# Attention, a cosine layer and a routed expert layer: the first layer from pairs of 256-token blocks to single blocks of 384 tokens, with weight bits in PSUM and a shorter gate

## Chip, cores, metric

The kernel runs on one core of one Trainium2 chip. The time is the device time of one execution in microseconds; it was run three times. A core has TensorE (matrix products, PE in the profile, its weight loads PEld), VectorE (DVE), ScalarE (ACT), GpSimd (POOL) and SyncE (SP), which here issues DMAs. Each engine works through its own queue in order.

## The reference

Three layers one after the other, all in float32:

```
x = attention(q, k, v)            # 4 batches, 8 heads, 576 positions, head size 64; the first 4 heads see a band
                                  # of 32 positions back, the last 4 see 32 positions in steps of 4
h = x @ w_in                      # 2304 tokens x 512 -> 2048
x = (h * cos(h)) @ w_out          # -> 512
logits = x @ w_gate + log1p(exp(x @ w_noise)) * noise      # 8 experts
top2, weights = the two largest of each token, softmax over them
out[token] += weight * relu(x @ w1[e]) @ w2[e]             # for both experts of a token; 512 -> 1024 -> 512
```

## The kernel before

**Precision.** A product in full float32 is made of three products in a faster float32 format: each operand is split into a rounded part and a rest (`PASSES`, L45), high with high, high with low, low with high. So every operand costs a rounding copy on ScalarE and a subtraction on VectorE or GpSimd. Small products (scores, transposes, gate) are plain float32; each of them, except the transposes, stands twice in the trace.

**Attention** is done in 16 units `u` (one batch and one pair of heads each): load, `a_scores` (L404), `a_exp`, `a_norm`, three transposes and the product with v (`a_part`, L525). Its result, already transposed, goes into a ring of 768 tokens in SBUF, `xraw`. Units 0 to 3 run in the opening; the others are laid beside the steps of the first layer. `x_split` (L540) cuts a block of the ring into the two parts.

**The first layer** works on 9 blocks of 256 tokens, and on pairs `p` of hidden chunks of 128 (8 pairs). A step (`g1`, `post`, `g2`) is: 24 products of 256 columns into one PSUM tile of 512; the cosine on it (ScalarE, VectorE, ScalarE twice, VectorE, ScalarE, GpSimd); and, two steps later, 12 products of 512 columns into the sums of the block's two tiles of tokens. The order of the 72 steps (L732) is: blocks 0 and 1 in turn through the 8 pairs (16 steps), then blocks 2 to 8 one after the other. PSUM has eight banks: two for `ph`, two for `mid` (attention), four with the tag `acc`, for the sums.

**Weights of the first layer** come as 64-bit words. `w_load` brings a piece of 512 KB (four a pair), `w_bits` (L282) puts each number together from its two words with three VectorE operations in place in SBUF (L290 to L292), `w_parts` rounds it on ScalarE (L298) and takes the rest on GpSimd (L299). Four pieces are cut in the opening, the other 28 during the first sixteen steps. The last pair comes over the small tiles `piece`.

**What sets the order.** The list `BESIDE` (L57) says, by step and place in it, which functions are issued there: `8:0` is after step 8's first cosine half and before the rest. The loop (L982) issues a step's first products, the cosine in three stretches and the second products of the step two before, with those functions in between.

**Routing** of a block of 256: `r_rows` writes the sums out, `r_trans` transposes them (8 transposes), `r_gate` (L617) makes partial gate sums of 32 rows for each quarter of the 512 features, `r_logits` transposes these (2) and adds them up; then softplus, the two largest, and `r_rank`, which gives each token its place in its experts' lists by products with a triangle of ones; `r_send` scatters number and weight into the list `tab` in DRAM, two indirect DMAs for each tile of 128 tokens.

**The experts.** Each expert has 608 places, as tiles of 128, 128, 96 (the first part, 352) and 128, 128 (the second part, 256). For an expert: gather and transpose the rows, 8 times 12 products with w1 for each part (`m_g1`, L891), 24 products of 512 columns for each tile with w2 (`m_y`, L928), scale, and add into the output rows by indirect DMA. Expert 0's first part is read from the lists before the last two blocks are routed (`t_first`, L830); its hidden layer runs while the last block is routed (L1015 to L1023). What follows needs the last block's entries.

Of the kernel before, what the change touches and what calls it, by code (L numbers as in the profile page):

```python
# [9 lines left out]
F32 = mybir.dt.float32  # L10
# [20 lines left out]
TB = 256  # L31
NBLK = NT // TB
NPAIR = DFF // 256
# [5 lines left out]
CAP = CA + CB  # L39
NEG = -8e9  # L40
TWO_PI = 2.0 * math.pi
RING = 3 * TB
# [11 lines left out]
)  # L54

# [30 lines left out]
9:1 w_bits(5,3)  # L86
9:2 a_part(6,0)
10:0 w_parts(5,2)
10:1 w_parts(5,3) w_piece(7,1) a_part(6,1)
# [3 lines left out]
11:1 a_exp(7) w_bits(7,0) w_parts(6,3)  # L93
12:-1 a_norm(7)
12:0 w_bits(7,1) w_parts(7,0) w_piece(7,2)
12:1 w_parts(7,1)
12:2 w_piece(7,3)
13:-1 a_loadv(7)
13:0 a_loadqk(8) a_part(7,0)
14:1 a_part(7,1)  # L100
14:2 w_bits(7,2) w_bits(7,3) x_split(2,0,2) a_part(7,2) w_parts(7,2)
15:-1 w_parts(7,3) x_split(2,2,3,1)
15:0 x_split(2,3,4,1)
16:0 a_loadv(8)
# [12 lines left out]
24:-1 a_part(8,1) r_logits(0)
24:0 zero_out(2)
24:1 a_part(8,2) r_trans(1)
25:-1 a_part(9,0)  # L120
25:0 r_exp(0) r_top(0)
25:2 a_scores(10)
26:-1 r_top2(0) r_gate(1) a_loadv(9) a_part(9,1)
26:0 zero_out(5) a_loadqk(11) r_rows(2) r_pick(0)
26:1 a_part(9,2) a_exp(10) a_norm(10) r_trans(2)
26:2 a_scores(11)
27:-1 a_loadv(10) zero_out(4) zero_out(6)
27:0 r_logits(1) r_gate(2) r_exp(1)
27:1 a_part(10,0) zero_out(7)
28:-1 a_part(10,1)  # L130
28:0 a_part(10,2) r_rank(0)
28:2 r_top(1) r_top2(1) r_send(0,0) a_exp(11)
29:-1 a_loadqk(12) a_norm(11)
29:0 a_loadv(11)
29:1 r_send(0,1)
29:2 r_pick(1) a_part(11,0)
30:-1 zero_out(9) a_part(11,1) zero_out(8) r_logits(2)
30:0 a_part(11,2)
30:1 r_exp(2)
30:2 a_loadv(12) x_split(4) zero_out(10) r_top(2) r_top2(2)  # L140
31:2 r_rank(1) zero_out(11) r_pick(2)
32:0 r_send(1,0)
32:2 r_send(1,1) zero_out(12)
33:2 zero_out(13) r_rank(2) r_rows(3)
34:0 r_send(2,0)
34:2 zero_out(14) r_send(2,1) r_trans(3)
35:2 zero_out(15) r_gate(3)
36:2 a_scores(12) zero_out(16)
37:0 a_loadqk(13)
37:2 a_exp(12) zero_out(17) r_logits(3)  # L150
38:1 a_norm(12) r_exp(3)
38:2 a_scores(13) x_split(5) r_top(3) r_top2(3)
39:0 a_part(12,0) a_loadqk(14)
39:2 a_part(12,1) a_exp(13) r_pick(3)
40:0 a_part(12,2)
40:1 a_norm(13)
40:2 a_loadv(13) a_scores(14)
41:0 a_part(13,0) a_loadqk(15)
41:2 a_part(13,1) a_exp(14) r_rank(3) r_rows(4)
42:0 a_part(13,2) r_send(3,0)  # L160
42:1 a_norm(14)
42:2 a_loadv(14) a_scores(15) r_send(3,1) r_trans(4)
43:0 a_part(14,0)
43:2 a_part(14,1) a_exp(15) r_gate(4)
# [1021 lines left out]
```

## Time and profile before

| | us |
|---|---|
| three timed runs | 1032.69, 1036.55, 1035.54; median 1035.54 |
| the profiled execution: its own time | 1032.98 |
| the profiled execution: span | 1031.2 |
| granted TensorE clock over the span | 0.984 of full speed |
| TensorE busy | 980.9 |
| VectorE, ScalarE, GpSimd busy | 547.5, 458.7, 368.1 |

"Busy" is the time in which an engine had at least one operation running; idle time stands beside the operation that followed it, with what ended the wait. The granted clock has two levels, 1.2 and 2.4 GHz; a mean of 0.93 says that a part of the stretch ran at the lower one.

### The profile page before, as it was taken

The page shows a single profiled execution, that of the slowest core. Times are in us where ns is not written, and L with a number is a line of the kernel's source. Part 1 is how long each engine was busy: PE and PEld are TensorE (multiplying, and loading weights), DVE is VectorE, ACT ScalarE, POOL GpSimd, SP SyncE. Part 2 cuts the span into 40 slices and gives each one's busy share as a digit, 9 for nine tenths or more (in the row PEclk, how much of TensorE's full clock was granted, in tenths as well). Part 3 has the DMA queues.
Part 4 walks back from the last instruction along what each step waited for, and adds up shares of the span by engine and source line. Part 5 has one row for each costly group of instructions (what it writes and reads, how often), then busy time and mean ns, then how long its engine had stood idle before and what let it go on. Part 6 is the DMA issues. An engine that isn't in the chain of part 4 may idle for free.

```text
span 1031.2 us, 16810 instructions
## 1 busy us (share of the span) xinstructions
PE 980.9 (95%) x6560; PEld 864.8 (84%) x6560; DVE 547.5 (53%) x1134; ACT 458.7 (44%) x908; POOL 368.1 (36%) x477
## 2 busy tenths in 40 slices
PE   8797989999999899999999889999999999999995
PEld 6676778988889788898887689898898979898984
DVE  7799885357754655354464556344453536353221
ACT  6646765555645655455554334233232414142110
POOL 5555553243453341323334432231313232322211
PEclk9998999999999999999999999999999999999998
DMA  9962212223312120000054345453434243441201
GB/s 216 328 220 81 80 55 43 85 72 114 96 52 57 40 55 1 21 1 23 21 192 122 84 134 176 140 168 110 156 126 157 76 154 124 157 149 55 67 26 47
DMA packets 70601, 105.19 MB, mean 102 GB/s; under 512 B 31251, under 2 KB 44819, under 8 KB 70512
## 3 DMA queue, kind: packets, MB, share of 16 engines
q1 hardware_dynamic: 60528, 76.34, 24.3%
q0 software_dynamic: 9984, 27.68, 8.7%
q8 instruction: 54, 0.88, 0.4%
q14 instruction: 35, 0.29, 0.1%
HBM read 85.41 MB, written 19.59 MB: 102 GB/s over the span
## 4 chain that ended last, share of the span: by engine, by line
PE 72%; DVE 13%; ACT 5%; DMA 4%; issue 3%; SPq 1%; POOL 1%; ACTq 0%; DVEq 0%; POOLq 0%
PE pe L903 20%; PE ye L938 20%; PE ph L562 13%; PE acc L589 12%; DVE cut L291 3%; DMA raw<-in_wm 2%; PE sc L430 2%; PE mgx L886 2%; DVE cut L290 1%; DVE cut L292 1%; DVE r L571 1%; PE mo L505 1%; DVE po L654 1%; PE mt L485 1%; DVE r L575 1%
## 5 line engine op out<-in xcount | busy, mean ns | idle before, releaser
L562 PE MATMUL ph<-xhl,wm 128*128 128x256 f32 x1728 | 230.0, 289 | 11.6 <-ACT wm L298 4.3
L562 PEld LDWEIGHTS ph<-xhl,wm 128*128 128x128 f32 x1728 | 219.4, 195 | 19.9 <-ACT wm L298 4.7
L938 PE MATMUL ye<-we,h 128*128 128x512 f32 (+1 forms) x960 | 231.0, 397 | 0.0
L589 PE MATMUL acc<-wm,g 128*128 128x512 f32 x864 | 220.3, 398 | 2.8 <-POOL wm L299 0.9
L938 PEld LDWEIGHTS ye<-we,h 128*128 128x128 f32 (+1 forms) x960 | 173.9, 184 | 43.3
L589 PEld LDWEIGHTS acc<-wm,g 128*128 128x128 f32 x864 | 156.8, 190 | 33.7 <-POOL wm L299 1.2
L579 POOL TENSOR_TENSOR g<-r,g 128x512 fp32r<-128x512 f32 x72 | 95.7, 1329 | 207.5 <-ACT g L578 207.4
L903 PE MATMUL pe<-xga,we 128*128 128x352 f32 x768 | 125.4, 323 | 0.0
L903 PEld LDWEIGHTS pe<-xga,we 128*128 128x128 f32 x768 | 122.7, 188 | 0.5 <-issue 0.4
L951 POOL DMA_INDIRECT out<-old,tir x35 | 35.6, 1017 | 221.9 <-DVE old L949 217.1
L906 DVE SCALAR_TENSOR_TENSOR h<-pe,h 128x256 fp32r<-128x256 f32 (+1 forms) x128 | 60.6, 474 | 97.1 <-ACT h L905 96.2
L905 ACT ACTIVATE h<-pe 128x256 fp32r<-128x256 f32 (+1 forms) x128 | 54.2, 424 | 122.2 <-PE pe L903 122.2
L949 DVE SCALAR_TENSOR_TENSOR old<-ye,wts,old 128x512 f32<-128x512 f32 (+1 forms) x35 | 26.3, 750 | 135.5 <-PE ye L938 135.5
L903 PE MATMUL pe<-xgb,we 128*128 128x256 f32 x768 | 95.9, 286 | 1.8 <-DVE xgb L889 1.3
L903 PEld LDWEIGHTS pe<-xgb,we 128*128 128x128 f32 x768 | 94.7, 195 | 2.5 <-DVE xgb L889 1.5
L571 DVE SCALAR_TENSOR_TENSOR r<-r,ph 128x512 f32<-128x512 int32 x72 | 49.1, 682 | 82.9 <-ACT r L570 82.8
L575 DVE SCALAR_TENSOR_TENSOR r<-r,ph 128x512 f32<-128x512 f32 x72 | 49.4, 686 | 82.2 <-ACT r L574 82.0
L820 DVE TENSOR_TENSOR we<-wraw,we 128x512 fp32r<-128x512 f32 x121 | 82.5, 691 | 3.6 <-ACT we L819 0.9
L819 ACT ACTIVATE we<-wraw 128x512 fp32r<-128x512 f32 x128 | 78.4, 623 | 3.2 <-issue 3.2
L573 ACT ACTIVATE r<-r 128x512 f32<-128x512 f32 x72 | 45.4, 631 | 65.5 <-DVE r L571 65.4
L570 ACT ACTIVATE r<-ph 128x512 int32<-128x512 f32 x72 | 42.6, 592 | 51.1 <-PE ph L562 50.9
L578 ACT ACTIVATE g<-r 128x512 fp32r<-128x512 f32 x72 | 45.4, 631 | 43.8 <-DVE r L575 29.5
(181 smaller groups left out, 1035.3 us busy)
## 6 DMA issues: line engine op xcount, KB each, us to landing
wraw<-in_we SPq DMA_DIRECT2D x64, 512.0 KB, 5.7
raw<-in_wm SPq DMA_DIRECT2D x28, 512.0 KB, 9.8
vts<-in_v SPq DMA_DIRECT2D x13, 384.0 KB, 3.9
x1d<-x SPq DMA_DIRECT2D x9, 512.0 KB, 3.6
out<-zt SPq DMA_DIRECT2D x18, 256.0 KB, 3.9
kts<-in_kT SPq DMA_DIRECT2D x13, 288.0 KB, 3.1
qts<-in_qT SPq DMA_DIRECT2D x26, 144.0 KB, 3.9
piece<-in_wm SPq DMA_DIRECT2D x4, 512.0 KB, 4.0
```

Of the source, the lines that this page charges most:

```text
L562: nc.tensor.matmul(ph[:, j, :], w[:, a, o:o + P], t[:, x, c, :], start=(c == 0 and n == 0 and (j == 0 or len(cs) == 4)), stop=(c == 3 and ...
L571: nc.vector.scalar_tensor_tensor(r, n, -TWO_PI, ph, op0=ALU.mult, op1=ALU.add)
L573: nc.scalar.activation(r, r, AF.Sin, scale=0.5)
L575: nc.vector.scalar_tensor_tensor(r, r, 0.5, ph, op0=ALU.subtract, op1=ALU.mult)
L579: nc.gpsimd.tensor_tensor(g[:, 1, :], r, g[:, 0, :].bitcast(F32), op=ALU.subtract)
L589: nc.tensor.matmul(ACC[blk][t], g[:, a, j * TB + t * P:j * TB + (t + 1) * P], w[:, x, 1024 + j * DM:1024 + (j + 1) * DM], start=(p == 0 an ...
L819: nc.scalar.activation(t[:, 0, fs], raw, AF.Copy)
L820: eng.tensor_tensor(t[:, 1, fs], raw, t[:, 0, fs].bitcast(F32), op=ALU.subtract)
L903: nc.tensor.matmul(ph[:, :n], w[:, a, o:o + P], x[:, b, c, :], start=(c == 0 and i == 0), stop=(c == 3 and i == 2))
L905: nc.scalar.activation(h[:, 0, f, :], ph[:, :n], AF.Relu)
L906: nc.vector.scalar_tensor_tensor(h[:, 1, f, :], ph[:, :n], 0.0, h[:, 0, f, :].bitcast(F32), op0=ALU.max, op1=ALU.subtract)
L938: nc.tensor.matmul(acc, h[:, a, f, o:o + n], w[:, b, (f % 4) * DM:(f % 4 + 1) * DM], start=(f == 0 and i == 0), stop=(f == 7 and i == 2))
```

## The change

- The first layer has 6 blocks of 384 tokens, and a step is one hidden chunk of 128 instead of two: 12 products of 384 columns, and, two steps later, 9 products of 512 columns into three sums. There are 96 steps, and the blocks run one after the other from the start.
- `x_split` works on one quarter of the features at a time, with six such tiles in turn.
- The four banks `acc` become four banks `k0` to `k3` that are given out by number. A block's three sums take three of them; the fourth serves its neighbour's routing, and, while weights are being cut, the intermediate of `w_bits`.
- The last pair of weights comes in eight pieces of half the size.
- For attention units 4 to 7, the scaling of the maxima and the copies of the result go from VectorE to ScalarE.
- The gate is one product per tile and quarter: the transposed rows are loaded, the 16 gate columns are streamed, and the four quarters add up in PSUM. `r_logits` goes away.
- Routing is done 6 times, for three tiles each.
- `t_first` reads the first parts of experts 0 and 1 before the last block is routed. Of expert 0's weights 14 of 16 splits run beside the steps. Expert 1's first rows are gathered while the last block is routed, and its first part's products stand before expert 0's second part.
- `BESIDE` is written anew from step 9 on.

```
-TB = 256
+TB = 384
-RING = 3 * TB
+RING = 2 * TB
...
     def w_bits(j, k):
...
+        b = bank(f"bits{j}_{k}", BITS[0]).bitcast(U32)[:, :n]
         V = nc.vector
-        V.tensor_scalar(t, hw, 3, 0x3FFFFFF8, op0=ALU.logical_shift_left, op1=ALU.bitwise_and)
-        V.scalar_tensor_tensor(t, hw, 0xC0000000, t, op0=ALU.bitwise_and, op1=ALU.bitwise_or)
-        V.scalar_tensor_tensor(t, lw, 29, t, op0=ALU.logical_shift_right, op1=ALU.bitwise_or)
+        V.tensor_scalar(b, hw, 3, 0x3FFFFFF8, op0=ALU.logical_shift_left, op1=ALU.bitwise_and)
+        V.scalar_tensor_tensor(b, hw, 0xC0000000, b, op0=ALU.bitwise_and, op1=ALU.bitwise_or)
+        V.scalar_tensor_tensor(t, lw, 29, b, op0=ALU.logical_shift_right, op1=ALU.bitwise_or)
...
+    def x_split(blk, c, eng=nc.vector):
+        t = bpool.tile([P, 2, TB], F32R, tag="xhl", name=f"xhl{blk}_{c}", bufs=6)
...
+    def g1(blk, f, cs=range(4)):
+        w, j = WM[f // 2], f % 2
...
+        for c in cs:
+            for n, (a, x) in enumerate(PASSES):
+                o = c * 256 + j * P
+                nc.tensor.matmul(ph, w[:, a, o:o + P], XHL[blk, c][:, x, :],
+                                 start=(c == 0 and n == 0), stop=(c == 3 and n == 2))
...
+    def g2(blk, f, ts=range(NTB)):
...
+        for t in ts:
+            for n, (a, x) in enumerate(PASSES):
+                nc.tensor.matmul(ACC[blk][t], g[:, a, t * P:(t + 1) * P],
+                                 w[:, x, 1024 + j * DM:1024 + (j + 1) * DM],
...
+    def r_gate(blk):
+        mid = r_bank(f"mg{blk}", blk)
+        for t in range(NTB):
             for c in range(4):
...
+                nc.tensor.matmul(mid[:, t * 2 * NE:(t + 1) * 2 * NE], RT[blk][t][:, c, :], wgn[:, c, :],
+                                 start=(c == 0), stop=(c == 3))
...
-    steps = [(blk, p) for p in range(NPAIR) for blk in range(2)]
-    steps += [(blk, p) for blk in range(2, NBLK) for p in range(NPAIR)]
+    steps = [(blk, f) for blk in range(NBLK) for f in range(NF)]
...
+    r_trans(LAST, 0)
+    r_trans(LAST, 1)
+    m_g1(0, 0, 0)
+    r_trans(LAST, 2)
+    split_we(0, 3, 2)
+    m_g1(0, 0, 1)
+    r_gate(LAST)
+    r_exp(LAST)
+    split_we(0, 3, 3)
     load_we(1, 0)
     load_we(1, 1)
+    m_g1(0, 0, 2)
+    r_top(LAST)
...
+    for t in range(3):
+        t_gather(1, t)
+    for f in range(5, 8):
+        m_g1(0, 0, f)
+    r_rank(LAST)
+    for t in range(NTB):
+        r_send(LAST, t)
+    for t in range(3):
+        m_y(0, t)
+        t_trans(1, t)
+        for q in range(3 * t, min(3 * t + 3, 8)):
+            split_we(1, q // 4, q % 4)
+    t_load(0, 2)
     t_gather(0, 3)
     t_gather(0, 4)
...
+    t_load(2, NE)
+    for f in range(8):
+        m_g1(1, 0, f)
+        if f == 5:
+            t_weights()
+            for t in range(3):
+                m_out(0, t)
     t_trans(0, 3)
     t_trans(0, 4)
```

## Rows read from the trace of the kernel before

**Rows 1.** The page, part 1: busy time, share of the span and instructions by engine

```profile
PE 980.9 (95%) x6560; PEld 864.8 (84%) x6560; DVE 547.5 (53%) x1134; ACT 458.7 (44%) x908; POOL 368.1 (36%) x477
```

**Rows 2.** Windows: stretch, length, busy PE, PEld, DVE, ACT, POOL; clock, DMA, GB/s

```profile
0.00:39.90 39.90, 34.26 (x355) 27.57 (x355) 28.10 (x63) 27.47 (x119) 20.45 (x49) 1.00 1.05 258
39.90:165.90 126.00, 109.06 (x766) 93.88 (x767) 110.31 (x149) 75.06 (x162) 71.07 (x57) 0.93 0.42 128
165.90:553.60 387.70, 379.28 (x2774) 335.56 (x2773) 205.25 (x550) 215.03 (x338) 140.43 (x164) 1.00 0.18 55
553.60:639.70 86.10, 79.12 (x462) 70.80 (x461) 48.09 (x111) 33.33 (x68) 34.53 (x48) 0.96 0.51 149
639.70:1031.20 391.50, 379.21 (x2208) 337.02 (x2206) 155.74 (x264) 107.78 (x224) 101.65 (x163) 0.99 0.35 114
```

**Rows 3.** Chain of waits: start us, us, what (instructions), single pieces of it

```profile
233.81 1.98 PE sc L430 x18
...
454.07 2.87 PE ph L562 x24
456.94 2.75 PE acc L589 x12
...
555.57 0.87 PE mx L613 x8
...
558.36 0.57 PE mg L621 x8
...
561.04 0.22 PE ml L630 x2
...
612.46 5.47 PE ye L938 x24
...
624.30 5.76 PE pe L903 x36
...
964.42 26.86 PE pe L903 x192
```

**Rows 4.** By line: duration ns min/median/max, first and last start, forms

```profile
L290 DVE TENSOR_SCALAR cut<-raw x28: 368/420/1521, 21.6 to 141.0; 128x512 uint32<-128x512 uint32 x28
...
L291 DVE SCALAR_TENSOR_TENSOR cut<-raw,cut x28: 691/1370/1685, 22.0 to 141.4; 128x512 uint32<-128x512 uint32 x28
...
L571 DVE SCALAR_TENSOR_TENSOR r<-r,ph x72: 627/686/689, 39.9 to 546.2; 128x512 f32<-128x512 int32 x72
```

**Rows 5.** Windows of what reads or writes `cut`: busy DVE, ACT, POOL

```profile
39.90:165.90 126.00, 81.44 (x84) 17.80 (x28) 36.95 (x29) 0.93 0.42 128
```

**Rows 6.** Waits of VectorE, 39.9 to 165.9: us in total, times, longest

```profile
DVE r L575 <- ACT r L574: 7.8, 6, 1.4
DVE r L571 <- ACT r L570: 5.9, 5, 1.6
```

**Rows 7.** Groups by line and shape: operations on 384 columns (busy us, mean ns)

```profile
L448 POOL TENSOR_TENSOR s<-s,mx 128x384 f32<-128x384 f32 x8 | 7.1, 886 | 0.1
...
L888 ACT ACTIVATE xga<-mgx 128x384 fp32r<-128x384 f32 x8 | 3.9, 490 | 28.6 <-PE mgx L886 28.6
L889 DVE TENSOR_TENSOR xga<-mgx,xga 128x384 fp32r<-128x384 f32 x8 | 4.4, 556 | 0.7
```

**Rows 8.** TensorE in order of time: start, us, what, idle before it

```profile
574.53 0.19 PE L693 MATMUL mr<-os,tri 128*128 128x8 bf16 x1 [3.73 <-DVE os L687]
...
592.06 0.66 PE L886 MATMUL mgx<-ident,xg 128*128 128x128 f32 x4 [0.30 <-DMA xg<-x1d,tic]
...
598.09 5.95 PE L903 MATMUL pe<-xgb,we 128*128 128x256 f32 x35 [1.32 <-DVE xgb L889]
```

**Rows 9.** GpSimd in order of time: start, us, what, idle before it

```profile
223.57 1.92 POOL L474 TENSOR_TENSOR s<-s,sm 128x288 f32<-128x288 f32 x3 [0.42 <-DVE sm L472]
...
577.08 1.17 POOL L714 DMA_INDIRECT tab<-pay,si  x1 [5.80 <-DVE si L707]
...
581.63 0.95 POOL L714 DMA_INDIRECT tab<-pay,si  x1 [0.23 <-issue]
```

More of the change, by code (lines that the diff above doesn't have):

```diff
@@ new lines @@
+47:-1 x_split(3,2)
+47:0 x_split(3,3)
+47:2 a_exp(14) a_loadqk(15)
+48:0 a_norm(14)
+49:0 a_part(14,0)
+49:2 a_part(14,1) r_rows(2)
+50:0 a_part(14,2) r_trans(2,0)
+50:2 a_scores(15) r_trans(2,1)
+51:0 r_trans(2,2) a_loadv(15)
+51:2 r_gate(2) a_exp(15)
+52:0 a_norm(15)
+52:1 r_exp(2)
+52:2 r_top(2) r_top2(2)
+53:0 a_part(15,0)
+53:2 a_part(15,1) r_pick(2)
+54:0 a_part(15,2) x_split(4,0)
+55:0 x_split(4,1)
+55:2 r_rank(2)
+56:0 r_send(2,0)
+56:2 r_send(2,1)
+57:0 r_send(2,2)
+63:-1 x_split(4,2)
@@ new lines @@
+63:0 x_split(4,3)
+65:2 r_rows(3)
+66:0 r_trans(3,0)
+66:2 r_trans(3,1)
+67:0 r_trans(3,2)
+67:2 r_gate(3)
+68:1 r_exp(3)
+68:2 r_top(3) r_top2(3)
+69:2 r_pick(3)
+70:0 x_split(5,0)
+71:0 x_split(5,1)
+71:2 r_rank(3)
+72:0 r_send(3,0)
+72:2 r_send(3,1)
+73:0 r_send(3,2)
+79:-1 x_split(5,2)
+79:0 x_split(5,3)
+81:2 r_rows(4)
+82:0 r_trans(4,0)
+82:2 r_trans(4,1)
+83:0 r_trans(4,2)
+83:2 r_gate(4)
+84:0 load_we(0,0)
+84:1 r_exp(4)
+84:2 r_top(4)
+85:0 r_top2(4)
+85:2 r_pick(4)
+87:0 r_rank(4)
+87:2 r_send(4,0) split_we(0,0,0)
@@ L204 @@
+88:0 r_send(4,1) split_we(0,0,1)
+88:2 r_send(4,2) split_we(0,0,2)
+89:0 split_we(0,0,3)
+89:2 t_first()
+90:0 split_we(0,1,0) load_we(0,1)
+90:2 split_we(0,1,1) t_gather(0,0) t_gather(0,1) t_gather(0,2)
+91:0 split_we(0,1,2)
+91:2 split_we(0,1,3)
+92:2 split_we(0,2,0)
+93:0 split_we(0,2,1)
+93:1 t_trans(0,0)
+93:2 split_we(0,2,2)
+94:0 split_we(0,2,3) t_trans(0,1)
+94:1 t_trans(0,2)
+94:2 split_we(0,3,0)
+95:0 split_we(0,3,1)
 """
@@ L718, in r_send @@
                 tc.declare_no_dep(d.ins, o.ins, reason="every slot is written once")
-            if blk >= NBLK - 2:
-                tc.declare_no_dep(d.ins, EARLY[0].ins, reason="expert 0's first slots are final")
+            for o in EARLY:
+                tc.declare_no_dep(d.ins, o.ins, reason="the first slots of the first experts are final")
             scat.append(d)
@@ L734 @@
-    extras = {}
-    def at_step(i, pos, f, *a):
-        extras.setdefault((i, pos), []).append((f, a))
-    def run(i, pos):
-        for f, a in extras.get((i, pos), []):
-            f(*a)
-    START = [-1, 3, 7, 11, 20, 22, 24, 26, 36, 38, 40, 42]
-    for u in range(4, FUSED):
-        at_step(START[u - 4] + 2, -1, a_norm, u)
-        at_step(START[u - 4] + 3, 0 if u == 4 else -1, a_part, u, 0)
-    pieces = [(0, 2), (0, 3)] + [(j, k) for j in range(1, NPAIR) for k in range(4) if (j, k) > (1, 1)]
@@ L995 @@
         if i >= 2:
-            g2(*steps[i - 2], range(1, 2))
+            g2(*steps[i - 2], range(1, NTB))
         run(i, 2)
+    assert not beside
     g2(*steps[-2])
-    for t in range(2):
-        r_send(NBLK - 2, t)
     g2(*steps[-1])
     LAST = NBLK - 1
+    nc.scalar.activation(one, one, AF.Exp)
     r_rows(LAST)
```

576 lines of the change are left out of this document (230 added, 346 removed), and 4 rows, old and new, of the table OPENING.

## The prediction

> **What bounds the kernel now.** I read the busy shares first. TensorE works 980.9 of 1031.2 us [rows 1], so only about 50 us are idle, and the question is where they lie. The table by stage [rows 2] answers it. Its five stretches are: the opening, to the first cosine step's start; the first sixteen steps of the first layer (39.9 to 165.9); its other 56 steps (to 553.6); the passage to the experts, up to the end of expert 1's first part; and the rest of the experts. In the third and fifth TensorE is busy 98 and 97% at a granted clock of 1.00 and 0.99: there only less work on TensorE helps. In the second it is busy 109.1 of 126.0 us at a mean clock of 0.93, and VectorE 110.3. In the fourth it is idle for 7 us, at a mean clock of 0.96.
>
> The chain of waits gives the prices of TensorE's products [rows 3]. 24 products of 256 columns take 2.87 us, 119.6 ns each; 12 of 512 take 2.75 us, 229.2 ns each. A step of before is one of each: 5.62 us. An expert's 96 products of 352 columns and 96 of 256 take 26.86 us, so one of 352 takes (26.86 - 11.48)/96 = 160.2 ns.
>
> In the second stretch the culprit is preparing the weights: its three bit operations per piece hold VectorE for 81.4 us [rows 5]. The middle one lasts 0.69 us at best and 1.69 at worst, whereas the cosine's operation of the same 512 elements, which reads one operand from PSUM, never goes above 0.69 [rows 4]. So the stretching falls on operations with both inputs in SBUF, beside GpSimd, and not on those with one in PSUM.
>
> **The change, part by part.** The profiled execution took 1032.98 us, 1.8 more than its span; the median of the three timed runs is 1035.54, 2.6 above it. The sum goes from 1032.98.
>
> *Products in steps of 384 tokens.* A product of 384 columns lies between 352 and 512: 160.2 + 32/160 x 69.0 = 174.0 ns (from 256 to 352 extended, 173.7; one and a half times the 256 price, 179.4, is the upper end, 170 a lower one). A step is 12 x 174.0 + 9 x 229.2 ns = 2.09 + 2.06 = 4.15 us, and there are 96 instead of 72: 398.4 against 404.6 us. But a block takes 16 steps, so after the sixteenth 80 steps remain, not 56: 80 x 4.15 - 56 x 5.62 = **+17.3 us** (-4 to +5). The second products that lag two steps behind are shorter by 2 x 0.69: **-1.4**.
> The Trainium skill ("TensorE: Matmul & The Clock Gate", Back-to-back issue gap) gives a gap of N/2.4 + 2.5 ns, 109.2 for 256 columns and 162.5 for 384. By that rule the larger product would save 1.4 us in all instead of 6.2. The rows show 119.6 where it says 109.2, so I keep the rows.
>
> *The first sixteen steps.* 16 x (5.62 - 4.15) = 23.5 us of TensorE's work leave this stretch for later, while all 28 pieces of weights stay in it. With 85.6 busy us left on TensorE (109.1 - 23.5), the stretch can't be much under 86. VectorE: with the intermediate in PSUM each of the three operations has at most one input in SBUF, so I take the 0.69 of [rows 4] for each, also for the first, which gets by with 0.42 now. 24 pieces x 3 x 0.69 = 49.7; the last pair's 8 half pieces, at 0.42 by the slope between 0.556 for 384 [rows 7] and 0.69 for 512, are 10.1; together 60 instead of 81.4. Of the other 28.9 us the cosine's two operations shrink by 32 x 0.13 = 4, the attention's copies and scalings, which go to ScalarE, take about 4.8 + 3.6 with them, and four splits for block 1 add some 3. That is 80 instead of 110.3 us. VectorE now has 15.7 us without work in the stretch, mostly between the cosine's halves, waiting for ScalarE [rows 6]; these waits stay, and ScalarE takes over about 5 us of copies, of which I give 4 to the path: 80 + 15.7 + 4 = 100 us, **-26**. Ends: 86 (TensorE's own work), and 113 if the three operations get no faster (97.6 + 15.7), so -40 to -13.
> The Trainium skill ("SBUF — State Buffer", Who interferes with whom) says that a VectorE instruction with at most one SBUF input outside the 2-port modes doesn't contend with GpSimd, which the two ranges of [rows 4] bear out. But its "VectorE: DVE Perf Modes", Why PSUM operands drop a tier, speaks against the edit: a PSUM operand takes the double rate away. The first operation's 0.42 against 0.69 us is that price, 0.27 x 32 = 8.6 us, already inside the 60.
>
> The opening: two splits of block 1 ahead of the first steps fall away; in this stretch VectorE isn't full. I take **-1** (-3 to 0).
>
> *Gate in one product.* Before: four products of the gate and two transposes, 0.57 + 0.22 us [rows 3]. After: 12 float32 products that load 128 columns each and stream 16. A float32 product stands twice in the rows; the scores, which load 128 columns and stream 96, take 1.98/18 = 0.11 us per row. Streaming less doesn't shorten the load, so 24 x 0.11 = 2.64 us a block; were it half, 1.32. On the path, five routings instead of eight: 5 x 2.64 - 8 x 0.79 = **+6.9 us** (0.3 to 6.9). Transposes: 60 instead of 64 of 0.11, **-0.4**. The ranks' few bf16 products, the shorter VectorE chain and the weights' loads are hidden behind the steps.
>
> *The passage.* From the first layer's last product to the end of expert 1's first part it takes 86.0 us [rows 2] (this part starts at 624.30 [rows 3] and has 8 x 1.92 us of products). TensorE's work of after: first parts of experts 0 and 1, 2 x 15.4; 12 transposes 1.3, gate 2.6, rank 0.3; five tiles of second products, 5 x 5.5; seven tiles' transposes 3.1; expert 0's second part 11.5: 77. Against it runs the chain through the routing. Before, the ranks came 20.9 us after the first layer's end, with 3.73 us of idleness in front, and the first gathered rows of expert 0's second part 38.4 us after it; its products started for good at 44.4 only, behind the weights of all tables on VectorE [rows 8]. After, VectorE has one stage fewer and leaves three quarters of the weights' splits to earlier steps, so the ranks should be ready when expert 0's eight products and the gate have run, about 19.5. Two sends more at 1.52 [rows 9] add 3.0, two table loads more 1.0: 38.4 - 1.4 + 3.0 + 1.0 = 41 us. TensorE reaches that point after 53, because expert 1's first part now lies in front. The 12 us are the cover; what the chain is late by beyond them comes back on the path. I take 79 (2 us for starts): **-7** (-9 to -2).
>
> Sum: +17.3 - 1.4 - 26 - 1 + 6.9 - 0.4 - 7 = -11.6; 1032.98 - 11.6 = **1021.4 us**.
>
> **Rivals.**
> *A, TensorE alone sets the first steps.* If the waits between the cosine's halves are covered too, the stretch falls to about 87 us: 1021.4 - 13 = 1008. For it: VectorE (80) and TensorE (86) both have room. Against it: ScalarE's 75 us in the same stretch don't shrink, and the waits lie in a fixed order.
> *B, the edit doesn't do what it says.* The operations that write PSUM, a form that the trace doesn't hold, stay as long as now, or TensorE's order fills with waits for ScalarE: 113 us, 1034.4, no change. For it: no row shows a PSUM write by VectorE. Against: the flat 0.69 of the cosine's operation.
> *C, the shorter step starves (slower).* A step's second products start two steps after its first: 11.2 us now, 8.3 after. The way through the cosine is, for 384 columns, 4 x 0.5 on ScalarE, 2 x 0.556 on VectorE, 1.0 on GpSimd (0.886 for a subtraction of 384 elements [rows 7]; gaps included about 4.5 us). That leaves 3.8 us. Normalising (1.92 us [rows 9]), subtracting in the scores, and sends (2 x 1.52) stand in front of it in GpSimd's queue in 31 of the 80 later steps, and they themselves wait for VectorE. Where burst and wait exceed 3.8 us, TensorE stops; if this is 0.9 us on average in those 31 steps, it costs 28 us: 1049. It decides from 0.37 us on average (11.6/31). For it: two steps carry a normalising and a send together, 5 us. Against: most bursts alone stay under 3.8.
> *D, the passage's cover is too short.* The weights of expert 1, 4 MB, are loaded in the passage itself; if its first part waits for them, the 7 us fall away: 1028.
>
> **How the numbers follow.** Forecast 0.48, A 0.17, B 0.14, C 0.13, D 0.08. About 0.5% is what a measurement of this kernel tells from no change, so faster is under 1030.4 and slower over 1040.7. Faster: forecast, A and D nearly whole, a little of B, 0.69. Same: most of B and the rims, 0.15. Slower: C and a rest of B, 0.16. The range 1004 to 1039: down to A with a cheap gate (1008 - 4), up past B; beyond lie the rest of A and most of C.
>
> **What would show it.** A step of 4.15 us in the chain; bit operations that never exceed 0.75 us; sixteen first steps in 100 us, VectorE's cut operations at 60; a gate of 2.6 us; no wait of TensorE for the ranks and none for the gathered rows of expert 0's second part. The prediction is wrong if the first stretch stays over 112 us, if steps behind the sixteenth show waits for GpSimd, or if TensorE stands before expert 1's first part.

## The result, and the profile after

The changed kernel takes 1045.3 us (median of 4 runs, 1044.4 to 1046.8), the kernel before 1035.36 us beside it: a ratio of 1.0101, interval 1.0077 to 1.0124. The same kernel run again (a0_after below) gave 1.0135 (1.0109 to 1.0161). The forecast was 1021.4 us, so it is wrong in sign. The profiled execution took 1044.4 us, its span 1042.7.

First the page's busy times of the changed kernel, against [rows 1]:

```profile
PE 994.9 (95%) x6047; PEld 878.4 (84%) x6047; DVE 513.4 (49%) x1096; ACT 472.4 (45%) x1019; POOL 353.9 (34%) x495
```

VectorE's busy time fell by 34 us, as intended, and TensorE's rose by 14. Where, the windows by stage tell, with the same five stretches and columns as [rows 2]: stretch, length, busy PE, PEld, DVE, ACT, POOL, granted clock, DMA, GB/s.

```profile
0.00:40.70 40.70, 35.09 (x336) 28.72 (x336) 26.84 (x60) 26.66 (x117) 19.74 (x47) 0.92 1.02 287
40.70:147.40 106.70, 91.21 (x551) 77.82 (x552) 79.81 (x142) 72.45 (x187) 57.88 (x59) 0.86 0.46 138
147.40:565.10 417.70, 407.55 (x2472) 360.87 (x2470) 206.81 (x516) 237.48 (x435) 149.93 (x189) 1.00 0.17 51
565.10:648.70 83.60, 79.30 (x482) 71.75 (x481) 38.26 (x107) 23.83 (x51) 17.63 (x32) 1.00 0.38 119
648.70:1042.70 394.00, 381.79 (x2208) 339.27 (x2208) 161.63 (x273) 111.97 (x232) 108.69 (x171) 0.99 0.37 121
```

| stretch | before | after | difference | forecast |
|---|---|---|---|---|
| opening | 39.9 | 40.7 | +0.8 | -1 |
| first sixteen steps | 126.0 | 106.7 | -19.3 | -26 |
| other steps of the first layer | 387.7 | 417.7 | +30.0 | +22.4 |
| passage | 86.1 | 83.6 | -2.5 | -7 |
| rest of the experts | 391.5 | 394.0 | +2.5 | 0 |

The forecast column is the sum's own: 17.3 - 1.4 + 6.9 - 0.4 = 22.4 for the other steps. Every stretch came out worse than forecast, by 1.8, 6.7, 7.6, 4.5 and 2.5 us, 23 in all; no single one of them makes the sign.

The operations themselves did what was foretold. The three bit operations by line (duration min/median/max), against [rows 4]:

```profile
L332 DVE TENSOR_SCALAR bits<-raw x28: 675/688/695, 21.3 to 118.9; 128x512 uint32<-128x512 uint32 x28
L333 DVE SCALAR_TENSOR_TENSOR bits<-raw,bits x28: 695/696/697, 22.0 to 119.6; 128x512 uint32<-128x512 uint32 x28
L334 DVE SCALAR_TENSOR_TENSOR cut<-raw,bits x28: 686/687/690, 22.8 to 120.4; 128x512 uint32<-128x512 uint32 x28
```

No operation leaves 0.69 us by more than 0.02, and VectorE is busy for 79.8 us in the first sixteen steps (forecast 80). And the chain of waits around the passage (start us, us, what), against [rows 3]:

```profile
565.81 1.09 PE mx L667 x8
566.90 1.94 PE pe L888 x12
568.84 0.44 PE mx L667 x4
569.28 1.94 PE pe L888 x12
571.21 2.58 PE mg L675 x24
573.80 2.06 PE pe L888 x12
...
579.99 6.11 PE pe L888 x36
586.10 0.22 PE mr L742 x9
...
976.07 27.16 PE pe L888 x192
```

The gate takes 2.58 us (forecast 2.64), and the ranks (mr) start without a wait, where 3.73 us of idle time stood in front of them before [rows 8]. The last line is an expert's 192 first products: 27.16 us, in [rows 3] 26.86.

What fills the 26.9 us in which VectorE is not busy in the first sixteen steps (106.7 - 79.8; forecast 19.7)? Its waits there (us in total, times, longest), against [rows 6]:

```profile
DVE r L619 <- ACT r L618: 10.0, 7, 2.9
DVE r L615 <- ACT r L614: 6.2, 7, 2.5
DVE sm L520 <- ACT s L509: 5.0, 2, 2.9
DVE cut L334 <- POOL wm L341: 2.6, 1, 2.6
```

All but the last are for ScalarE. The two between the cosine's halves, 16.2 us together, are not much above the 13.7 of [rows 6]; what came in is the wait for the exponentials (5.0 us where it was 1.4) and the one behind GpSimd (2.6, where there was none). ScalarE's own order of time shows why (start us, us, engine, line, operation; one attention unit's exponentials; of nine pairs the first and the last line stand):

```profile
68.80 1.28 ACT L509 ACT_TABLE_LOAD   x1
70.09 0.34 ACT L509 ACTIVATE s<-sc,mx 128x96 f32<-128x96 f32 x1
70.33 0.19 ACT L509 ACTIVATION_READ_ACCUMULATOR s<-sc,mx 128x1 f32 x1
...
72.85 0.25 ACT L509 ACTIVATION_READ_ACCUMULATOR s<-sc,mx 128x1 f32 x1
72.94 0.67 ACT L340 ACTIVATE wm<-cut 128x512 fp32r<-128x512 f32 x1
73.46 0.54 ACT L614 ACTIVATE r<-ph 128x384 int32<-128x384 f32 x1
74.02 1.28 ACT L617 ACT_TABLE_LOAD   x1
```

From 68.8 to 75.3 ScalarE does nothing for the cosine but its first operation (0.54): a table load of 1.28 us, nine exponentials with their sums, a weights' piece, and a second table load for the sine. A step lasts 4.19 us now. TensorE stands behind this burst and behind those of the next two units (the third time by a detour: GpSimd is late with its part of a piece of weights, VectorE's bit operations wait for it, and ScalarE for those). Ahead of them it stands once where step 2's products wait for a free bank of `ph` (order of time, idle before in brackets):

```profile
43.89 2.61 PE L607 MATMUL ph<-xhl,wm 128*128 128x384 f32 x7 [3.24 <-DVE r L619]
...
73.67 0.98 PE L607 MATMUL ph<-xhl,wm 128*128 128x384 f32 x2 [2.95 <-ACT wm L340]
...
102.13 1.51 PE L534 MATMUL mt<-ident,s 128*96 128x128 f32 x6 [3.12 <-ACT r L614]
...
127.72 0.74 PE L632 MATMUL acc<-wm,g 128*128 128x512 f32 x2 [2.34 <-ACT g L622]
```

and the granted clock falls behind them (windows, columns as above; clock third from the end):

```profile
70.00:80.00 10.00, 6.68 (x23) 5.19 (x22) 5.66 (x12) 8.60 (x30) 5.31 (x6) 0.69 0.65 180
100.00:110.00 10.00, 7.87 (x47) 7.07 (x48) 6.90 (x12) 8.11 (x21) 6.41 (x7) 0.66 0.05 19
...
130.00:140.00 10.00, 8.89 (x41) 7.18 (x41) 5.07 (x12) 7.09 (x14) 4.34 (x7) 0.57 0.71 154
```

In the last of these TensorE counts as 89% busy, but at a mean clock of 0.57 its products run at the lower of the two levels for most of the time. Over the whole stretch the clock is 0.86, before it was 0.93 [rows 2].

The trace of the kernel before had a sign of this. It has the same three bursts with the same six table loads in this stretch, and behind the first of them TensorE stood there too:

```profile
83.07 0.80 PE L562 MATMUL ph<-xhl,wm 128*128 128x256 f32 x2 [3.34 <-ACT wm L298]
```

Right behind the other two no wait there was longer than 0.9 us. Now all three stop TensorE for 2.3 us or more.

### The profile page after: what moved, and what is told of

Same layout as the page of the kernel before. It is cut to its first block, busy times and chain, and to the rows that moved or that the text cites. A ratio compares the mean times of both kernels' runs of the same rounds, so it can differ in the third digit from the quotient of the medians.

```text
span 1042.7 us, 15952 instructions
## 1 busy us (share of the span) xinstructions
PE 994.9 (95%) x6047; PEld 878.4 (84%) x6047; DVE 513.4 (49%) x1096; ACT 472.4 (45%) x1019; POOL 353.9 (34%) x495
## 4 chain that ended last, share of the span: by engine, by line
PE 68%; DVE 13%; ACT 8%; issue 4%; POOL 3%; DMA 2%; SPq 1%; DVEq 0%; ACTq 0%; POOLq 0%
PE ye L923 21%; PE pe L888 20%; PE ph L607 11%; PE acc L632 9%; PE mgx L872 2%; DVE r L615 1%; DVE bits L333 1%; DVE bits L332 1%; PE mg L675 1%; ACT r L617 1%; DVE r L619 1%; ACT r L618 1%; PE sc L476 1%; POOL tab L760 1%; DVE cut L334 1%
## 5 line engine op out<-in xcount | busy, mean ns | idle before, releaser
L607 PE MATMUL ph<-xhl,wm 128*128 128x384 f32 x1152 | 230.6, 349 | 8.2 <-DVE r L619 4.3
L632 PE MATMUL acc<-wm,g 128*128 128x512 f32 x864 | 230.9, 405 | 5.8 <-POOL g L623 3.3
L623 POOL TENSOR_TENSOR g<-r,g 128x384 fp32r<-128x384 f32 x96 | 97.1, 1013 | 220.1 <-ACT g L622 219.5
L890 ACT ACTIVATE h<-pe 128x352 fp32r<-128x352 f32 (+1 forms) x128 | 54.2, 424 | 131.2 <-PE pe L888 131.2
L891 DVE SCALAR_TENSOR_TENSOR h<-pe,h 128x352 fp32r<-128x352 f32 (+1 forms) x128 | 60.7, 475 | 98.4 <-ACT h L890 97.7
L615 DVE SCALAR_TENSOR_TENSOR r<-r,ph 128x384 f32<-128x384 int32 x96 | 53.0, 552 | 104.5 <-ACT r L614 104.5
L619 DVE SCALAR_TENSOR_TENSOR r<-r,ph 128x384 f32<-128x384 f32 x96 | 52.8, 550 | 84.5 <-ACT r L618 84.5
L622 ACT ACTIVATE g<-r 128x384 fp32r<-128x384 f32 x96 | 50.2, 523 | 68.5 <-DVE r L619 55.0
L617 ACT ACTIVATE r<-r 128x384 f32<-128x384 f32 x96 | 50.2, 523 | 55.9 <-DVE r L615 55.5
L614 ACT ACTIVATE r<-ph 128x384 int32<-128x384 f32 x96 | 46.6, 486 | 58.2 <-PE ph L607 51.6
```

The costliest lines, as they stand in the source:

```text
L607: nc.tensor.matmul(ph, w[:, a, o:o + P], XHL[blk, c][:, x, :], start=(c == 0 and n == 0), stop=(c == 3 and n == 2))
L615: nc.vector.scalar_tensor_tensor(r, n, -TWO_PI, ph, op0=ALU.mult, op1=ALU.add)
L617: nc.scalar.activation(r, r, AF.Sin, scale=0.5)
L619: nc.vector.scalar_tensor_tensor(r, r, 0.5, ph, op0=ALU.subtract, op1=ALU.mult)
L623: nc.gpsimd.tensor_tensor(g[:, 1, :], r, g[:, 0, :].bitcast(F32), op=ALU.subtract)
L632: nc.tensor.matmul(ACC[blk][t], g[:, a, t * P:(t + 1) * P], w[:, x, 1024 + j * DM:1024 + (j + 1) * DM], start=(f == 0 and n == 0), stop=(f ...
```

## The experiments

Sixteen runs were made, each beside the kernel before on the same chip. The table has their stretches, worked out from start times in the traces: the first sixteen steps from ScalarE's first operation of step 0 to the first product of step 16 (0.6 us longer than the windows above), the passage from the first layer's last product to the first product of expert 1's second part. One expert's time is the same for each of experts 2 to 7 (but for a single one of e14, 57.11).

| kernel | to before, interval | first 16 steps | other steps | passage | an expert |
|---|---|---|---|---|---|
| before | 1 | 126.7 | 387.3 | 86.2 | 56.69 |
| changed | 1.0101 (1.0077-1.0124) | 107.3 | 417.3 | 84.0 | 57.02 |
| a0_after, the same again | 1.0135 (1.0109-1.0161) | 107.3 | 417.6 | 83.9 | 57.02 |
| e1_square | 1.0076 (1.0051-1.0101) | 101.6 | 420.4 | 84.0 | 57.02 |
| e2_oldgate | 1.0074 (1.0047-1.0100) | 106.5 | 409.7 | 84.5 | 56.83 |
| e2b_oldgate_pad | 1.0071 (1.0053-1.0088) | 107.2 | 410.2 | 84.8 | 57.02 |
| e3_bits_sbuf | 1.0329 (1.0304-1.0354) | 128.8 | 420.5 | 83.9 | 57.02 |
| e4_passage | 1.0204 (1.0190-1.0217) | 108.0 | 420.0 | 90.9 | 57.02 |
| e8_common_max | 1.0140 (1.0119-1.0161) | 107.1 | 423.0 | 86.2 | 56.69 |
| e11_norm_late | 1.0141 (1.0126-1.0157) | 108.2 | 416.7 | 83.9 | 57.02 |
| e13_pad | 1.0109 (1.0091-1.0127) | 108.1 | 418.2 | 83.7 | 56.69 |
| e14_ph_mid | 1.0129 (1.0114-1.0144) | 107.7 | 421.4 | 85.5 | 57.02 |
| e15_step_alone | 1.0284 (1.0263-1.0306) | 128.7 | 410.0 | 89.0 | 56.83 |
| e7_gate_before | 1.0084 (1.0061-1.0108) | 126.8 | 394.6 | 88.6 | 56.69 |
| e9_before_bits | 0.9963 (0.9950-0.9975) | 123.5 | 386.7 | 86.3 | 56.69 |
| e9b_bits_apart | 0.9924 (0.9904-0.9944) | 119.2 | 387.7 | 84.6 | 56.69 |
| e12_before_passage | 1.0031 (1.0016-1.0046) | 127.2 | 387.4 | 86.8 | 56.67 |
| e6_before_both | 1.0003 (0.9989-1.0017) | 123.8 | 386.8 | 87.9 | 56.67 |

The stretches come from one profiled execution each, the ratios from all runs. The opening differs by up to 5 us between executions of kernels that have the same opening (38.5 to 43.7 among those built on the kernel before), so a single span decides nothing under some 5 us. The first sixteen steps are steadier, 107.3 us in both executions of the changed kernel; its other steps take 416.7 to 423.0 us in the variants that leave the gate as it is. The same kernel run again missed its own expectation, 1.0135 where 1.008 to 1.012 was expected.

**Undoing and doing one part.**

```diff
 e3_bits_sbuf (changed kernel)
-        b = bank(f"bits{j}_{k}", BITS[0]).bitcast(U32)[:, :n]
+        b = t
```

> The changed kernel with the intermediate of the bit operations back in SBUF (written in place), and nothing else. Theory S and my forecast agree on VectorE: the middle operation goes back to durations between 0.69 and 1.7 us and VectorE is busy about 95 us instead of 79.8 in the first sixteen steps. They differ in what that costs: by the forecast, where VectorE sets the stretch, it becomes 110 to 116 us and the time 1050 to 1055; by theory S, where ScalarE's bursts set it and VectorE has 27 us of room, the stretch stays under 109 us and the time within 3 us of 1045.

Both expectations were too small: the stretch is 128.7 us. The middle operation by line, and the window of the stretch:

```profile
L333 DVE SCALAR_TENSOR_TENSOR cut<-raw,cut x28: 691/1643/1758, 21.7 to 135.8; 128x512 uint32<-128x512 uint32 x28
```

```profile
38.30:167.00 128.70, 100.02 (x554) 82.30 (x553) 104.41 (x142) 73.23 (x188) 68.20 (x60) 0.81 0.40 122
```

Without the edit the operation is dearer than before (median 1.64 against 1.37 us), VectorE is busy for 104.4 us, and the stretch is VectorE's busy time plus 24.3. With the edit it is 79.8 plus 26.9. So 24.6 us of VectorE's work are worth 21.5 us of the stretch: it does go with that work, and theory S, by which VectorE has room, is refuted in that form.

```diff
 e15_step_alone (changed kernel, with the edits of e2, e3 and e4)
```

> The changed kernel with three of its four parts taken back: the intermediate of the bit operations in SBUF, the old gate, expert 1's first part behind expert 0's second. What is left is the first layer in steps of 384 tokens, one block at a time. Theory D (the shorter step moves TensorE's work out of the stretch that VectorE sets, so that VectorE's time stays and the work comes on top later): the first sixteen steps take about 128 us as before, the other steps about 410 instead of 387, the passage about 90: 1060 to 1065. By my forecast's sum (steps +17.3 - 1.4, the first sixteen steps -13 at least): at most 1038.

Theory D holds in every number: 128.7, 410.0 and 89.0 us, 1063.0 in all, 29 us more than the kernel before. The window of the stretch:

```profile
41.00:169.70 128.70, 98.81 (x555) 81.40 (x554) 104.39 (x142) 73.25 (x188) 68.25 (x60) 0.83 0.42 124
```

The shorter step takes 16 x (5.62 - 4.19) = 22.9 us of TensorE's work out of the stretch, and the stretch does not get shorter (126.7 before), because the work of VectorE stays in it. TensorE's work comes on top later: 387.3 to 410.0, of which 80 x 4.19 - 56 x 5.62 = 20.5 are the steps. This kernel keeps what came with the step: the order of the blocks, the copies on ScalarE, the half pieces, the new `BESIDE`. What each of these is worth by itself no run shows.

```diff
 e9_before_bits (kernel before)
+            b = psum.tile([P, 512], F32, tag="mid", name=f"bits{j}_{k}", bufs=2).bitcast(U32)
-        V.tensor_scalar(t, hw, 3, ...
+        V.tensor_scalar(b, hw, 3, ...
 e9b_bits_apart: as e9, but eleven pieces instead of three stay in SBUF
```

> The kernel before with one part of the change alone: the bit operations of 21 of the 24 pieces prepared beside the first sixteen steps put their intermediate into PSUM (a turn of the two banks that the attention uses; three pieces that fall between scores and exponentials stay in SBUF). Steps, gate and passage are those of before. Theory V (VectorE's instructions plus its waits for ScalarE set the first sixteen steps): VectorE's busy time there falls by about 21 x (2.91 - 2.07) = 18 us from 110, its waits stay near 16 to 22, the stretch falls from 126 us to 110 to 116 and the time by 10 to 16 us against the kernel before. Rival P: TensorE has 109 us of work in this stretch and loses as much to the clock as before, and the shared banks add waits: the stretch stays over 120 and the time within 5 us of before.

> The kernel before with the intermediate of 13 of 24 pieces in PSUM: of the 21 pieces of the earlier kernel, the 8 whose operations stand between an attention unit's transposes and products stay in SBUF. There VectorE's longest wait was 5.0 us and TensorE waited 11 us in all for banks that both use. If the shared banks held back the gain, the first sixteen steps take 118 to 121 us (123.5 with 21 pieces, 126.7 without) and the time is 0.990 to 0.994 of before. If VectorE's relief is simply not worth more beside TensorE's 109 us of work, they take 124 to 126 and the time is 0.996 to 1.000.

(The counts in these two are wrong: of 28 pieces, 25 and 17 are in PSUM.) With 25 pieces the stretch is 123.5 us, the rival's number; with 17 it is 119.2 and the kernel takes 1026.7 us, 0.9924 of before: it beats both kernels. Fewer relieved pieces win more, as was expected if the shared banks held the gain back. The window of e9b's stretch:

```profile
42.50:161.70 119.20, 104.39 (x767) 91.88 (x768) 93.89 (x149) 75.78 (x164) 65.37 (x58) 0.96 0.44 134
```

VectorE: 93.9 us busy and 25.3 without work, before 110.3 and 15.7 [rows 2]. So 16.4 us less work is worth 7.5 us (126.7 to 119.2) with the long step.

```diff
 e7_gate_before (kernel before)
-            nc.tensor.matmul(mid[32 * c:32 * c + 32, :TB], wgn[:, c, :], xt[:, c, :], start=True, stop=True)
+            nc.tensor.matmul(mid[:, :2 * NE], xt[:, c, :P], wgn[:, c, :2 * NE], start=(c == 0), stop=(c == 3))
...
 (and the block's second 128 tokens in the same way in place of the transposes)
 e2_oldgate, e2b_oldgate_pad (changed kernel)
-                nc.tensor.matmul(mid[:, t * 2 * NE:(t + 1) * 2 * NE], RT[blk][t][:, c, :], wgn[:, c, :],
+                nc.tensor.matmul(mid[32 * c:32 * c + 32, t * P:(t + 1) * P], wgn[:, c, :], RT[blk][t][:, c, :],
...
 (then the copy, the transposes and the sum over the four groups, as in the kernel before)
```

> The kernel before with the new gate alone: each block's tokens are the loaded operand, 4 float32 products of 128 tokens each stream 16 columns (the other half of the block takes the place of the old transposes, so nothing else moves). By my account 16 records of 0.11 us replace 0.79 us a block: 1.75 us, nine blocks, +8 to +9 us: about 1044. If streaming 16 columns were half as dear it would be +1 or less (1036); if the gate lies in gaps of TensorE, no change (1035).

> The changed kernel with the old gate: 16 gate columns padded to 32 as the loaded operand, four groups of 32 rows of PSUM written one beside the other, then a copy, three transposes and a sum over the four groups. My account: the gate costs 2.62 us of TensorE a block in the changed kernel; the old form on 384 tokens costs about 24 records of 0.04 to 0.07 us and three transposes of 0.11, 1.3 to 1.9 us; six blocks, so the time falls by 4 to 8 us (1037 to 1041). Rival: the gate's products fill gaps that TensorE has anyway, and the longer chain (copy, transposes, sum) gives the gain back in the passage to the experts: within 2 us of 1045.

> The changed kernel with the old gate, and with two unused columns that shift the tiles' addresses. By the steps of the traces a block's gate costs 1.4 us less (a step with the third transposes and the gate 5.59 + 0.41 us later, instead of 7.29 + 0.09): six blocks 8.3 us; if the shift brings experts 2 to 7 from 56.83 to 56.69 again, 1 us more. So 7 to 10 us under the changed kernel beside it. If the medians of the earlier call were right, 3 us.

> The changed kernel once more, as the measure for the runs beside it on the same chip: 1.008 to 1.012 of before.

The first came out as worked out: 1042.6 us beside 1033.4, +9.2. e2 came out within its range (1039.9 us). Taken out of the changed kernel in e2b, the gate is worth 5.8 us by the medians beside each other (1040.7 and 1046.5), less than the 7 to 10 expected, and 7.4 us in the other steps by the traces (417.6 to 410.2), 1.5 a block. The chain of the old gate on 384 tokens, in e2b, ahead of which the same products stand as above:

```profile
562.62 1.93 PE pe L903 x12
564.56 0.79 PE mg L681 x24
```

0.79 instead of 2.58 us, and three transposes more. The passage doesn't gain from it (84.8).

```diff
 e4_passage (changed kernel): m_g1(1, 0, f) moved from ahead of t_trans(0, 3) into expert 1's own turn
 e12_before_passage (kernel before): the changed kernel's passage on blocks of 256; e6_before_both: with e9's edit
```

> The changed kernel with expert 1's first part taken out from beside the last routing and put back behind expert 0's second part; its tokens are still fetched early. By my account this takes 15.4 us of cover away from the chain that ends with the gathered rows of expert 0's second part: they are ready 41 us after the first layer's end, TensorE reaches that point after about 41 us without expert 1's first part. If the account is right, TensorE stands there for 3 to 8 us and the time rises by as much (1047 to 1052 where the changed kernel takes 1044). If the gathered rows come in time anyway, the time stays within 2 us of 1044, and the move of expert 1's first part is worth nothing.

> The kernel before with one part of the change alone: expert 1's first three tiles are fetched early and its first part runs beside the last routing, ahead of expert 0's second part. Blocks of 256 tokens, gate and bit operations as before. Theory P1 (the move fills TensorE's waits in the passage): the passage loses its 7 us of idleness and its two stretches at half clock, and falls from 86.1 to about 79; the time falls by 5 to 8 us against the kernel before (0.992 to 0.995). Theory P2 (what the changed kernel wins in the passage comes from its 384-token blocks, which leave 16 instead of 8 steps to split expert 0's weights): here the splits of experts 0 and 1 crowd ScalarE and VectorE, and the time falls by less than 2 us.

> The kernel before with two parts of the change and without the other two: the passage of the last kernel and the bit operations of 21 pieces in PSUM. If the parts add, the time is that of the passage alone less 4 us (the bit operations alone gave 0.9963 of before): by P1 0.988 to 0.991 of before, 1022 to 1025; by P2 about 0.995.

In the changed kernel the move is worth 7 us of passage (90.9 to 84.0). TensorE in e4's passage, idle before in brackets:

```profile
609.80 0.63 PE L872 MATMUL mgx<-ident,xg 128*128 128x128 f32 x4 [2.08 <-DMA xg<-x1d,tic]
611.42 0.63 PE L872 MATMUL mgx<-ident,xg 128*128 128x128 f32 x4 [0.99 <-DMA xg<-x1d,tic]
613.88 0.58 PE L888 MATMUL pe<-xgb,we 128*128 128x256 f32 x1 [1.83 <-ACT xgb L874]
617.68 7.51 PE L888 MATMUL pe<-xgb,we 128*128 128x256 f32 x41 [3.22 <-DVE xgb L875]
```

The first layer ends at 568.4 there, so the first gathered row is used 41.4 us later; the prediction's chain said 41. TensorE stands for 8.1 us there, the top of what was expected. On the kernel before the same move wins nothing and costs 0.3% (1038.5 beside 1034.6 us). TensorE stands 4.3 us for the ranks in the passage (3.7 before), and later, in expert 1's second part, 2.9 us for gathered rows, where there was no wait before (waits of e12, first from 553.6 to 650, then from 645 to 710):

```profile
PE mr L695 <- DVE os L689: 4.3, 1, 4.3
...
PE mgx L889 <- DMA xg<-x1d,tic: 2.9, 1, 2.9
```

That part of expert 1 takes 46.6 us there instead of 41.0, so the loss lies behind the passage (86.8). P2 named the splits as the reason: beside the last 8 steps of the kernel before only six of expert 0's sixteen are done, fourteen beside the changed kernel's last 16. That this is what makes the difference isn't shown. With the bit operations added (e6) the time is 1.0003 of before, outside both expectations; the two parts about add up (1.0031 and 0.9963).

**Inside the first sixteen steps.**

```diff
 e1_square
-            nc.scalar.activation(s[:, i, :], s3[i // 5][:, i % 5, :], AF.Exp, scale=0.125, ...
+            nc.scalar.activation(s[:, i, :], s3[i // 5][:, i % 5, :], AF.Exp if u < 5 else AF.Square, scale=0.125, ...
```

> The changed kernel, but ScalarE takes Square instead of Exp for the three attention units whose scores fall among the first sixteen cosine steps (units 5, 6, 7); this leaves their true exponential out, so that no table has to be switched from the sine's to the exponential's and back (two loads of 1.28 us per unit). Theory S: since VectorE has been relieved, ScalarE's bursts for these units (about 6 us: two table loads and nine exponentials with their sums) are longer than what a 4.2 us step leaves free, TensorE stops behind each of them for 2.3 to 3.1 us and then runs on at half clock. Then the stretch of the first sixteen steps falls from 106.7 us to 95 to 100, the stops right behind the units' scores shrink to under 1 us each, and the time falls by 6 to 11 us against the changed kernel (about 1036). Rival V: the stretch is set by VectorE and by TensorE's own order, and the bursts are hidden: the stretch stays within 2 us of 106.7 and the time within 3 us of 1045.

```profile
41.30:142.90 101.60, 86.53 (x555) 71.58 (x555) 79.89 (x142) 64.69 (x182) 58.09 (x59) 0.95 0.50 149
```

Six table loads, 7.7 us of ScalarE, are worth 5.7 us of the stretch (107.3 to 101.6), and the clock there rises from 0.86 to 0.95. It is one execution, but well outside the others: the changed kernel's two and the seven variants that keep both the bit operations in PSUM and the table loads lie between 106.5 and 108.2. VectorE's work is untouched at 79.9, its waits fall to 21.7. By the time as a whole the gain is not clear (1.0076 against 1.0101 and 1.0135; the other steps took 3 us longer in this execution). So the switching of tables is most of what the stretch lacks to the forecast 100, but not all.

```diff
 e8_common_max: two exponentials with one maximum a row instead of nine; VectorE sums
 e11_norm_late
-5:-1 a_exp(5) w_parts(3,1) w_load(5,0) a_norm(5) w_load(5,1) w_bits(3,2)
+5:-1 a_exp(5) w_parts(3,1) w_load(5,0) w_load(5,1) w_bits(3,2) a_norm(5)
 (and the same for unit 6)
 e14_ph_mid: step 1's sum in one of the attention's banks
```

> The changed kernel; units 5 to 7 take one maximum per row of the tile instead of one per row and window, so that two exponentials without sums replace nine with them, and VectorE sums the 864 elements afterwards. ScalarE's burst falls from about 5.5 to 3.6 us (both table loads stay), VectorE gets 0.9 us a unit more. Theory S (ScalarE's burst): the stretch of the first sixteen steps falls by 3 to 6 us from 107. Theory V: the sums on VectorE take back what the burst gives, and the stretch stays within 2 us of 107.

> The changed kernel with the order of two attention units changed alone: the normalising of units 5 and 6, in which VectorE stands for the exponentials for 5.0 us in all, comes behind the bit operations that follow it. Theory V: VectorE fills these 5 us with bit operations, and the first sixteen steps fall from 107 to 102 to 104 us. Theory S: TensorE stands for ScalarE's burst all the same, and the stretch stays within 1.5 us of 107.

> The changed kernel; only the sum of the second cosine step of the first block goes into one of the attention's two banks, so that the third step's products needn't wait for the first step's cosine (3.2 us in the profile of the changed kernel, the first wait of the stretch, with half clock behind it; the kernel before had a bank for it, which the fourth sum bank's new use took). If this wait is a cost of its own, the stretch falls from 107 by 3 to 6 us and the time by as much. Rival: VectorE and ScalarE, which are behind at that point, set the pace, and the wait only moves to a later step: within 1.5 us.

None of the three shortens the stretch: 107.1, 108.2 and 107.7 us. That is what the rival of each had said (theory V in e8, theory S in e11). In e8 ScalarE has 5.8 us less and VectorE 4.3 more, and nothing is won. In e11 VectorE's wait for the exponentials fell from 5.0 to 0.6 us, but its waits between the cosine's halves rose from 16.2 to 20.0, and TensorE waited 4.5 us for the transposes of the later normalising:

```profile
PE mt L534 <- POOL s L523: 4.5, 2, 4.4
PE ph L607 <- DVE r L619: 4.2, 2, 3.0
PE ph L607 <- ACT wm L340: 3.0, 1, 3.0
```

I read this as one chain through ScalarE and VectorE: a wait filled in one place comes back in another as long as the work of the two together doesn't shrink. In e8 it shrank by 1.5 us, in e1 by about 8. Nor does the stretch follow TensorE's clock: e8 and e11 have a mean of 0.92 there, the changed kernel 0.86, at the same length.

```diff
 e13_pad (changed kernel)
+        pad = small.tile([P, 1], F32, tag="pad", name=f"pad{n}", bufs=2)
+        nc.vector.memset(pad, 0.0)
```

> The changed kernel with two unused columns of 4 bytes set to zero at the start, which shifts the addresses of the tiles behind them and the program by two VectorE instructions, and nothing else. In the changed kernel each of experts 2 to 7 takes 57.02 us, in the kernel before 56.69, in the kernel with the common maximum 56.69, in that with the old gate 56.83, always the same to the hundredth within a kernel. If the price of a product hangs on where the program or its tiles lie, an expert takes another of these times here; if it hangs on the change's own instructions, it stays at 57.02.

An expert takes 56.69 us instead of 57.02 with two unused columns in front. The chain's row for one expert's first products, which was 27.16 in the changed kernel:

```profile
977.88 26.87 PE pe L892 x192
```

The stretch from expert 1's second part on takes 391.9 us instead of 394.0. So some 2 of the 2.5 us that the rest of the experts lost hang on where the program or its tiles lie, not on the change's own instructions. In e2b the same columns, behind a larger table of the gate, brought 57.02 again. Which address it is stays open.

## Why the prediction was wrong

- **The step that failed: "80 + 15.7 + 4 = 100".** VectorE's work is what the stretch goes with (e3, e15, e9b), and the 80 was right (79.8). The waits were carried over from a kernel with steps of 5.62 us, 15.7, with 4 added for copies; they are 26.9. With a step of 4.19 us ScalarE's bursts of some 6 us stop the other engines: e1 shows the table loads in them to be worth 5.7 us. [rows 6] shows no wait for the exponentials, and VectorE's was 1.4 us in all; TensorE's 3.34 us behind the first burst was there to be read and was not priced. That is rival B's second half, at 107 instead of 113. This step is 6.7 of the 23 us; with it put right the sum would have come to 1028, still the wrong sign, and the other terms below bring the rest.
- **The end at 113 failed in the same way.** It was to hold if the operations got no faster, 97.6 + 15.7. The 97.6 are 110.3 less what the cosine and the copies give up; the 3 us of splits and the 4 us of copies on the path, which the forecast counts, are left out, and with them it is 120.3. e3 shows 104.4 + 24.3 = 128.7. So the -26 has its source right, VectorE's relief, but the shorter step without it is far dearer than the sum's terms say: e15 takes 1063.0 us where they allow 1038 at most, 29 us more than the kernel before. Of this the bit operations give back 21.5 us in the stretch (e3) and the early first part of expert 1 four to seven in the passage (e2b beside e15, e4). On the kernel before the bit operations are worth 3 to 8 us of the stretch (e9, e9b), and the early first part nothing (e12). The change repairs with two parts what its first part costs, and pays for the gate besides.
- **Other steps, +30.0 instead of +22.4.** The gate was sized right: 5 x 2.58 - 8 x 0.79 = 6.6 us for the 6.9. A step takes 4.19 us instead of 4.15, 80 x 0.04 = 3.2 us: a product of 384 columns costs 175.5 ns where 174.0 was interpolated, and one of 512 costs 231.2 where it was 229.2. TensorE's idle time is 10.2 instead of 8.4 us, and one place at half clock came in, right behind the first block's gate; the following window holds it:

```profile
170.00:180.00 10.00, 10.00 (x51) 9.34 (x51) 4.53 (x12) 6.00 (x11) 3.57 (x5) 0.83 0.00 1
```

  It costs 1.7 us by its clock, (1 - 0.83) x 10. That leaves about 1 us not traced. The balance holds for this execution: a0_after, as long here (417.6), has no such place and 11.6 us of idle time. All that the larger product saves, 72 x 5.62 - 96 x 4.19 = 2.4 us, is less than the forecast 6.2, nearer to the 1.4 that the prediction set aside, and less than the gate costs.
- **Passage, -2.5 instead of -7.** The chain's 41 us and the cover were right (e4), the ranks came in time. TensorE's work is 79.3 instead of 77, and its idle time 4.3 instead of 2; 2.8 of that are starts behind copied rows.
- **Rest of the experts, +2.5 instead of 0.** No row of the prediction could show it; e13 shows some 2 us of it to hang on the layout.
- **Rivals.** C, the step that starves, decides from 11.6 us of waits; TensorE waits for GpSimd for 5.2 us in the other steps (3 x acc 2.7, 3 x mt 2.5), 2.2 in those before. The sign that the prediction gave for it came, but 3.0 us more are far below what decides, so it isn't the cause, though the sign of the result was C's. A failed for the same reason as the forecast. D didn't come: no wait for expert 1's weights.
- **Still open.** Of the 6.7 us in the first sixteen steps e1 explains 5.7 in one execution each. What the rest is isn't told apart; the copies that went to ScalarE, priced at 4 us, were not tried by themselves. The three attempts at the order say only that single waits can't be taken out.

## What to carry to other kernels

A shorter step saves nothing in a stretch that another engine sets: its work moves to where TensorE is full, and only what relieves the other engine brings it back, so price each part on the kernel with the other parts, not on the one before. When a step shrinks, list every burst on every engine that is longer than the new slack; waits read from the old trace are those that the old step let through. And before a larger rebuild, try its cheapest edit alone: the bit operations in PSUM, on 17 pieces of the old kernel, give 0.9924, which the whole change doesn't reach.

## What the runs showed of the hardware

- Two forms of float32 products that give the same 16 logits for 384 tokens cost 2.58 us with the tokens as the loaded operand and 0.79 (and three transposes more) with the gate's columns in four groups of 32. With 128 columns loaded a record takes 0.11 us, whether it streams 16 columns (here) or 96 (the scores, 1.98 us for 18 [rows 3]); with 32 loaded and 128 streamed 0.033. Whether the smaller load or the four groups side by side make the second form cheap, no run tells apart.
- A bit operation with both inputs in SBUF went from 1.37 us at the median to 1.64 in e3, where the step beside it is shorter; with the intermediate in PSUM it takes 0.70 in the changed kernel and on the kernel before (e9). GpSimd is the partner, by the start times in the traces: in e3 the 4 of 28 that run without a GpSimd operation beside them take 0.69 us, the other 24 have a median of 1.66; with the intermediate in PSUM it is 0.70 either way. The Trainium skill's "SBUF — State Buffer", Who interferes with whom, says that an instruction of VectorE with at most one input in SBUF, outside the 2-port modes, doesn't contend with GpSimd, and the trace agrees.
- The same products of an expert make it take 56.67, 56.69, 56.83 or 57.02 us, the same to the hundredth within a kernel but for one of e14 (57.11), and a change as small as eight bytes ahead of its tiles, with the two instructions that set them, moved 57.02 to 56.69.
